# One comparison per candidate builds the one-hot rows, and candidate columns are kept batch by batch

## The chip, the core and the metric

The kernel runs on one core of one Trainium2 chip. The metric is the device time of one execution in microseconds (us); lower is better. A core has five engines with a queue of instructions each: TensorE (PE; PEld is its weight load), VectorE (DVE), ScalarE (ACT), GpSimd (POOL) and SyncE (SP, which here only issues DMAs). An engine works through its own queue in order and waits, at the head of the queue, for what another engine or a DMA has to deliver.

## What is computed

Block-causal attention over 8 batches, 8 heads, 576 positions and 64 columns a head, and behind it a mixture of 8 experts over the 4608 tokens, each of which goes to one expert. An expert takes at most 80 tokens, those with the greatest gate weights; every other row of the output is zero. Cut to what matters:

```python
scores = np.where(mask, scale * q @ k.T, -1e9)
x = softmax(scores) @ v                      # 4608 tokens x 512
expert_idx = np.argmax(x @ w_gate, axis=1)
gate_w = probs[np.arange(N), expert_idx]
for e in range(8):
    tok_idx = np.where(expert_idx == e)[0]
    if len(tok_idx) > capacity:              # capacity is 80
        keep = np.argpartition(-gate_w[tok_idx], capacity)[:capacity]
        tok_idx = tok_idx[keep]
    h = np.maximum(x[tok_idx] @ w1[e], 0.0)
    out[tok_idx] = gate_w[tok_idx, None] * (h @ w2[e])
```

## The kernel before

There are three stages.

**Attention.** 32 pairs of heads, four to a batch (batches 0 to 7), go through a software pipeline. A hand-written table (TURN, and LAST for the last pair) says in which order each engine gets its instructions. DVE takes the maxima of the scores (`max`, L693), transposes q and k (`prep`, L633) and copies PSUM; ACT takes the exponentials (`soft`, L704) and starts on a tile when `merge` (L697, DVE) has set its shift; TensorE is fed by both. Between these steps the table has slots `t`, each of which puts one step of the router on DVE: the steps of a batch stand in a list (`enqueue`), and a slot takes the next one. For the last three batches the list is: reciprocals of the sums (`recip`, L400 to L405), products with the logits (L467) and their sum `lg` (L473), maximum, first index, weight, and `placed` (L579), which writes the batch's gate weights into `Wt`. The attention's result x goes to the DRAM tensor `xs` (`store_x`, L423), for the last batch when all of it has been transposed.

**Selection** (L976 to L1134). `Wt` holds on each of 128 partitions two halves of 160 columns; a partition stands for one of 8 experts and one of 16 token residues. `max` (L981) finds the best eight of each half, of which six are kept as candidates, `max_index` (L1011) their columns. `spread` (L991) and TensorE (L1004) bring every candidate of an expert to all 16 partitions of that expert, and 12 counts (six on DVE, L1049, six on ACT, L1053) say how many others are greater: the slot of the candidate. From the slot a one-hot row of 80 is made (`OH`, L1060, by `one_hot`, three candidates to an instruction). `pick` (L1079) is the matmul of the one-hot rows with the token numbers (`RI`); its reduction `gi` (L1083) is the list of tokens. POOL then gathers the tokens' x from `xs`, one indirect DMA for each expert (L1094, `xg`), the first three at once. A second matmul (L1120) with `RG` picks the gate weights (`gsum`, `comb`). `warm(n, ...)` (L796) puts n matmuls on TensorE whose result nobody reads; the list WARM says how many stand at each place, and WARM_PICK two more.

**Experts.** For the first expert DVE divides the gathered rows into four tiles `xn0_0` to `xn0_3` (`prepare_pieces`, L1203), TensorE transposes them (L1271), ACT copies (L1272), and the first matmuls follow (L1223). For the second expert `split` does the same division into a tile `xn` (also L1203). `finish` (L1136 to L1185) makes a check and the row numbers for the scatter. The loads of further weights are issued on SP behind the first gather.

From the selection on, the order is not written by hand: a scheduler places the instructions by its own estimate of when each can start, except where `issue_after` forces one behind another. The divide of the first expert is so forced behind `comb` (L1134); the divide of the second expert (`split`) is not.

Of the kernel before, what the change touches and what calls it, by code (L numbers as in the profile page):

```python
# [7 lines left out]
F32 = mybir.dt.float32  # L8
F32R = mybir.dt.float32r
BF16 = mybir.dt.bfloat16  # L10
# [12 lines left out]
WARM = [8, 8, 5, 9, 8, 9]  # L23
START_WARM = 6
WARM_PICK = 2
# [163 lines left out]
def tile_attn_moe(ctx, tc, q, k, v, w_gate, w1, w2, capacity, out, xs=None, dbg=None):  # L189
# [87 lines left out]
    iota_s = const.tile([P, CHUNK], F32, name="iota_s")  # L277
    iota_p = const.tile([P, 1], F32, name="iota_p")
# [109 lines left out]
    class Batch:  # L388
# [189 lines left out]
        def placed(self):  # L578
            yield nc.vector.tensor_scalar(  # L579
                Wt[:, :, :, self.b, :].rearrange("p h t a -> p t a h"),  # L580
                self.tp[:, 0:8 * NT].rearrange("p (t a h) -> p t a h", t=NT, h=2),
                scalar1=-SHIFT, scalar2=None, op0=ALU.add)


    Wt = sel.tile([P, 2, NT, 8, 4], F32, name="Wt")
    if B < 8:
        nc.vector.memset(Wt, -SHIFT)
    Wf = Wt.rearrange("p h t b a -> p (h t b a)")
    NW = NT * 64
    HW = NW // 2  # L590

# [196 lines left out]
    def warm(n, wt, after=None):  # L788

        if not n:  # L790
            return
        with ExitStack() as order:
            if after is not None:
                order.enter_context(tc.issue_after(after.ins))
            for i in range(n):
                last = nc.tensor.matmul(wt.rearrange("p (a c) -> p a c", c=P), lhsT=identr,  # L796
                                        rhs=identr.unsqueeze(1).broadcast_to([P, 4, P]), start=(i == 0),
                                        stop=(i == n - 1))
        return last
# [86 lines left out]
    with tc.manual_schedule():  # L886
# [43 lines left out]
        bt.flip(NP - 1, 0, 8)  # L930
        pairs[n - 1].take("V01", "a")
# [12 lines left out]
        bt.store_x()  # L944
# [35 lines left out]
    for h in range(2):  # L980
        vec.max(cand16[:, h], Wf[:, h * HW:(h + 1) * HW])  # L981

# [3 lines left out]
    near = sel.tile([P, 2, NCAND], F32, name="near")  # L986
# [22 lines left out]
    with tc.issue_after(spreads[-1].ins):  # L1009
        for h in range(2):  # L1010
            vec.max_index(cidx[:, h], cand16[:, h], Wf[:, h * HW:(h + 1) * HW])  # L1011
# [4 lines left out]
    pool.tensor_tensor(pen, pen, iota_c[:, 0:NH].unsqueeze(1).broadcast_to([P, 2, NH]), op=ALU.add)  # L1016
    pool.tensor_scalar(pen[:, 1], pen[:, 1], scalar1=8.0 * NCAND, scalar2=1.0, op0=ALU.add, op1=ALU.mult)

    part = sel.tile([P, 3, 2, NH], I32, name="part")
    cix = cidx[:, :, 0:NH].bitcast(I32)  # L1020
    vec.tensor_scalar(part[:, 0], cix, scalar1=5, scalar2=None, op0=ALU.logical_shift_right)
    vec.tensor_scalar(part[:, 1], cix, scalar1=2, scalar2=7, op0=ALU.logical_shift_right, op1=ALU.bitwise_and)
    vec.tensor_scalar(part[:, 2], cix, scalar1=3, scalar2=None, op0=ALU.bitwise_and)
    part = part.rearrange("p k h i -> p k (h i)")
    lo_ = sel.tile([P, NCAND], F32, name="lo_")
    hi_ = sel.tile([P, NCAND], F32, name="hi_")
    RI = sel2.tile([P, NCAND, 3, E], BF16, name="RI")
    RG = sel2.tile([P, NCAND, 3, E], BF16, name="RG")
    pool.tensor_scalar(lo_, part[:, 2], scalar1=32.0, scalar2=iota_r, op0=ALU.mult, op1=ALU.add)
    pool.tensor_scalar(lo_[:, NH:], lo_[:, NH:], scalar1=16.0, scalar2=1.0, op0=ALU.add, op1=ALU.mult)  # L1030
    for k, m in ((0, 2.0 * BLK), (1, float(S))):
        pool.tensor_scalar(near[:, k], part[:, k], scalar1=m, scalar2=(-float(BLK), 0.0)[k], op0=ALU.mult, op1=ALU.add)
    pool.tensor_tensor(hi_, near[:, 0], near[:, 1], op=ALU.add)
# [5 lines left out]
    per_expert(RI[:, :, 0], hi_)  # L1039
    per_expert(RI[:, :, 1], lo_)  # L1040
    pool.tensor_copy(RI[:, :, 2], sb)

    slot = sel.tile([P, NCAND], F32, name="slot")
# [13 lines left out]
    pen_ = pen.rearrange("p h i -> p (h i)")  # L1057

    def one_hot(c0, c1):
        return vec.tensor_tensor(OH[:, c0:c1], slot[:, c0:c1].unsqueeze(2).broadcast_to([P, c1 - c0, CHUNK]),  # L1060
                                 iota_s.unsqueeze(1).broadcast_to([P, c1 - c0, CHUNK]), op=ALU.is_equal)
# [13 lines left out]
    for i in range(NCAND):  # L1075
        with ExitStack() as order:
            if i == NV:
                order.enter_context(tc.issue_after(warm(WARM_PICK, wt[:, 1], picked).ins))
            picked = nc.tensor.matmul(pick[0:CHUNK, 0:3 * E], lhsT=OH[:, i], rhs=RI[:, i].rearrange("p k e -> p (k e)"),  # L1079
                                      start=(i == 0), stop=(i == NCAND - 1))  # L1080
# [64 lines left out]
    def finish_():  # L1145
# [10 lines left out]
        vec.tensor_tensor(chk[:, E:E + 2], slot[:, NH - 1:NCAND:NH], cap.broadcast_to([P, 2]), op=ALU.is_lt)  # L1156
# [225 lines left out]
    with tc.If(again > 0):  # L1382
# [10 lines left out]
        many = gen.tile([P, NW], BF16, name="many")  # L1393
# [176 lines left out]
```

## Time and profile before

| | us |
|---|---|
| median of 3 runs (382.64 to 382.75) | 382.7 |
| the profiled execution | 382.09 |
| its span, first to last instruction | 380.4 |

| engine | busy us | share of the span |
|---|---|---|
| PE | 366.7 | 96% |
| DVE | 285.9 | 75% |
| ACT | 286.9 | 75% |
| POOL | 181.0 | 48% |

The profiled execution took 1.7 us more than its span: that lies before the first and after the last instruction. A busy share is a mean over three stages with different limits, and in the selection TensorE is kept busy by matmuls that nobody reads, so the table does not say what sets the end; the views of the section after next do.

### The profile page before, as it was taken

What the parts mean: (1) busy time and instruction counts of PE and PEld (TensorE: products, weight loads), DVE (VectorE), ACT (ScalarE), POOL (GpSimd) and SP (SyncE); (2) the same over time, 40 slices, a digit from 0 to 9 for tenths busy, and PEclk for the clock granted to TensorE, in tenths of its full rate; (3) what the DMA queues carried; (4) which work ended last, traced back from release to release, by engine and by line L of the source; (5) the groups of instructions that cost most, each with busy time, mean ns of one, the idle gap of its engine ahead of it and who ended that gap; (6) DMA issues with size and microseconds to landing.
All of it is one profiled execution on the core that took longest, in us unless ns stands there. A gap on an engine that the chain in (4) does not pass through costs nothing.

```text
span 380.4 us, 15167 instructions
## 1 busy us (share of the span) xinstructions
PE 366.7 (96%) x5973; PEld 247.5 (65%) x5973; DVE 285.9 (75%) x804; ACT 286.9 (75%) x880; POOL 181.0 (48%) x373
## 2 busy tenths in 40 slices
PE   5899999999999999999999999999999999999993
PEld 3666667676676776676676676667667555666661
DVE  5889999999999999999999999999985311111001
ACT  1799999999999999999999999999521332322331
POOL 6346665656976766786577664431133112220000
PEclk9999999999999999999999999999999999999998
DMA  9979999999999999999999999999965999999940
GB/s 125 155 122 157 141 163 152 204 188 124 190 228 146 200 197 198 165 146 247 167 171 215 184 155 137 244 396 416 264 127 175 385 391 393 401 397 393 407 188 26
DMA packets 166272, 84.42 MB, mean 222 GB/s; under 512 B 132509, under 2 KB 151805, under 8 KB 166192
## 3 DMA queue, kind: packets, MB, share of 16 engines
q1 hardware_dynamic: 154768, 61.80, 75.4%
q0 software_dynamic: 9056, 21.27, 23.9%
q8 instruction: 49, 0.80, 1.0%
q10 hardware_dynamic: 2368, 0.30, 0.6%
q14 instruction: 31, 0.25, 0.3%
HBM read 63.21 MB, written 20.33 MB: 220 GB/s over the span
## 4 chain that ended last, share of the span: by engine, by line
PE 85%; DVE 8%; ACT 3%; DMA 2%; issue 1%; POOL 0%; POOLq 0%; ACTq 0%; SPq 0%; DVEq 0%
PE bank L764 21%; PE bank L657 20%; PE bank L738 13%; PE av L1321 9%; PE ps L1236 9%; PE bank L432 2%; PE bank L769 2%; DMA ld<-in_q_dram 2%; ACT P L704 2%; DVE raw L693 2%; DVE negm L693 1%; PE ps L796 1%; PE bank L674 1%; PE pm L1321 1%; DVE T L633 1%; PE bank L446 1%
## 5 line engine op out<-in xcount | busy, mean ns | idle before, releaser
L704 ACT ACTIVATE P<-bank,negm 128x512 f32<-128x512 f32 (+3 forms) x320 | 157.2, 546 | 9.1 <-DVE negm L693 5.8
L657 PE MATMUL bank<-T,qt 64*128 64x320 f32 (+3 forms) x512 | 98.8, 494 | 0.1
L764 PE MATMUL bank<-PT,vn 128*64 128x64 f32 (+3 forms) x1288 | 88.9, 292 | 0.0
L693 DVE TENSOR_REDUCE negm<-bank 128x1 f32<-128x320 f32 (+2 forms) x192 | 83.3, 472 | 6.2 <-PE bank L683 6.1
L786 ACT COPY PT<-bank 128x512 f32<-128x512 f32 x149 | 77.0, 633 | 3.3 <-PE bank L738 2.8
L764 PEld LDWEIGHTS bank<-PT,vn 128*64 128x64 f32 x1288 | 57.1, 137 | 26.8 <-ACT PT L786 3.4
L640 POOL TENSOR_SCALAR qt<-T 128x128 f32<-128x128 f32 (+2 forms) x96 | 31.1, 342 | 89.3 <-DVE T L633 89.3
L738 PEld LDWEIGHTS bank<-ident,P 64*128 64x128 f32 (+1 forms) x1600 | 57.9, 137 | 11.7 <-issue 6.6
L738 PE MATMUL bank<-ident,P 64*128 64x64 f32 (+1 forms) x1600 | 63.4, 225 | 1.3 <-ACT P L704 0.6
L657 PEld LDWEIGHTS bank<-T,qt 64*128 64x128 f32 x512 | 47.9, 187 | 25.4 <-ACT PT L786 15.8
L704 ACT ACTIVATION_READ_ACCUMULATOR P<-bank,negm 128x1 f32 x256 | 61.0, 238 | 0.0
L693 DVE TENSOR_REDUCE raw<-bank 128x1 f32<-128x64 f32 (+1 forms) x128 | 51.7, 443 | 2.2 <-PE bank L657 1.9
L633 DVE STREAM_TRANSPOSE T<-ld 128x576 f32<-128x576 f32 x64 | 49.0, 765 | 2.8 <-DMA ld<-in_q_dram 1.6
L626 POOL DMA_DIRECT2D vn<-in_v_dram x58 | 45.8, 792 | 0.6 <-issue 0.4
L1321 PE MATMUL av<-w,hT 128*32 128x512 f32 (+3 forms) x320 | 39.3, 554 | 0.0
L618 POOL DMA_DIRECT2D ld<-in_k_dram x54 | 37.4, 699 | 2.7 <-DMA ld<-in_q_dram 2.7
L1330 DVE SCALAR_TENSOR_TENSOR y<-av,comb,yt 80x512 f32<-80x512 f32 (+1 forms) x8 | 5.6, 696 | 42.0 <-ACT yt L1328 41.9
L1236 PE MATMUL ps<-xsT,w 128*64 128x80 f32 x896 | 32.6, 233 | 0.0
L1236 PEld LDWEIGHTS ps<-xsT,w 128*64 128x64 f32 x896 | 31.4, 138 | 1.4 <-issue 0.9
L1336 POOL DMA_INDIRECT out_dram<-y,si x8 | 7.5, 942 | 51.9 <-DVE y L1330 38.8
L1328 ACT ACTIVATE yt<-ps,gfar 32x512 f32<-32x512 f32 (+2 forms) x18 | 11.4, 634 | 24.5 <-PE ps L1321 24.4
L786 DVE COPY PT<-bank 128x512 f32<-128x512 f32 x43 | 29.2, 682 | 0.3
(203 smaller groups left out, 421.2 us busy)
## 6 DMA issues: line engine op xcount, KB each, us to landing
w<-in_moe_w_dram SPq DMA_DIRECT2D x13, 2048.0 KB, 15.8
xs<-Y SPq DMA_DIRECT2D x32, 288.0 KB, 6.4
out_dram<-zero SPq DMA_DIRECT2D x18, 512.0 KB, 8.2
ld<-in_q_dram SPq DMA_DIRECT2D x126, 72.0 KB, 5.3
vn<-in_v_dram POOLq DMA_DIRECT2D x58, 128.0 KB, 4.9
w<-in_moe_w_dram POOLq DMA_DIRECT2D x12, 512.0 KB, 7.2
ld<-in_k_dram SPq DMA_DIRECT2D x72, 72.0 KB, 5.1
ld<-in_k_dram POOLq DMA_DIRECT2D x54, 72.0 KB, 6.2
```

Source lines behind the costliest of these rows:

```text
L618: eng.dma_start(self.nat[x][r], (q, k)[x][b, h0 + h, :, 32 * i:32 * i + 32] .rearrange("(g r) d -> r g d", r=32))
L626: eng.dma_start(self.vn[:, h], v[b, h0 + h, 0:512].rearrange("(j p) d -> p j d", p=P))
L633: nc.vector.transpose(t, self.nat[x].rearrange("p g d -> p (g d)"))
L640: nc.gpsimd.tensor_scalar(qb[:, to], tb[:, of], scalar1=SCALE, scalar2=1.0, op0=ALU.mult, op1=ALU.mult)
L657: nc.tensor.matmul(s[h][:, c:c + n], lhsT=q_[:, P * t - BLK:P * t + BLK], rhs=k_[:, 0:n], start=(c == 0 and g != "2"), stop=(g == "1"))
L693: nc.vector.tensor_reduce(to[:, b, h:h + 1], self.s[g][h][:, c:c + n], axis=AX.X, op=ALU.max, negate=True)
L704: nc.scalar.activation(Pt[self.i % 2][u][:, h, c1:c1 + n], self.s[g][h][:, c:c + n], AF.Exp, bias=self.negm[:, t, h:h + 1], scale=1.0, acc ...
L738: nc.tensor.transpose(pt[c][0:cols.stop - cols.start, n_ * BLK:(n_ + 1) * BLK], row[u][r, h, cols], ident[r, r])
L764: nc.tensor.matmul(a4[r] if c0 is None else av[r, BLK * c0:BLK * (c0 + b1 - b0)], lhsT=self.vn[:, h, j, :], rhs=self.PT[:, h, row, b0:b1]. ...
L786: (nc.scalar.copy if (eng or TAKE[x]) == "a" else nc.vector.tensor_copy)(*self.out.pop(x))
L1236: last = nc.tensor.matmul(dst(b)[64 * c:64 * (c + 1)], lhsT=w_[:, a, cols], rhs=x_[a], start=(a == 0), stop=(a == n - 1))
L1321: last = nc.tensor.matmul(to[col:col + s1 - s0, c0:c1], lhsT=hT[:, a, s0:s1], rhs=w_[:, a, c0:c1], start=(a == ends[0]), stop=(a == ends[1 ...
```

## The change

- The columns of `Wt` are kept batch by batch, 18 to a batch, so a half is 144 columns wide, and a column number times 32 plus the residue is the token: the arithmetic that took a column number apart (`part` on DVE, `near`, `lo_`, `hi_` on POOL) becomes one multiplication (`at`).
- When batch 5 has been placed, two more `max` find the best eight of the first six batches of each half and write them behind the 144 columns. The last `max` then reads 44 columns (two batches and those eight).
- A one-hot row is made by one instruction for each candidate, twelve instead of four with two `slot` sums ahead: `iota - count == penalty`, with the iota as bf16. The constants for it are made once, in `constants3` (seven POOL instructions and one on DVE). `finish` makes the two `slot` values that it needs itself.
- The last batch's x is stored in two parts, the first right after its transposition.
- WARM has fewer matmuls at three places, WARM_PICK is gone.

```diff
-WARM = [8, 8, 5, 9, 8, 9]
+WARM = [8, 8, 3, 7, 8, 5]
-WARM_PICK = 2
...
+    def best_early():
+        for h in range(2):
+            yield nc.vector.max(Wt[:, h, HW:HW + 8], Wt[:, h, 0:NB * early_b])
...
             fill(bt.placed, "t2")
+            if bt.b == early_b - 1:
+                fill(best_early)
...
         bt.flip(NP - 1, 0, 8)
+        bt.store_x(0, 8)
...
         bt.flip(NP - 1, 8, S // 32)
-        bt.store_x()
+        bt.store_x(8)
...
-        vec.max(cand16[:, h], Wf[:, h * HW:(h + 1) * HW])
+        vec.max(cand16[:, h], Wt[:, h, NB * early_b:])
...
-    vec.tensor_scalar(part[:, 0], cix, scalar1=5, scalar2=None, op0=ALU.logical_shift_right)
...
+    pool.tensor_scalar(at.rearrange("p (h i) -> p h i", h=2), cidx[:, :, 0:NH].bitcast(I32), scalar1=32.0, scalar2=1.0,
+                       op0=ALU.mult, op1=ALU.mult)
...
-    hot = vec.tensor_tensor(slot[:, 0:NV], cnt_v, pen_[:, 0:NV], op=ALU.add)
-    for c0 in (0, 3):
+    hot = counted
+    for i in range(NCAND):
+        h, c = divmod(i, NH)
         with tc.issue_after(hot.ins):
-            hot = one_hot(c0, c0 + 3)
...
+            hot = vec.tensor_scalar(OH[:, i], iota_b[:, h], scalar1=(cnt_v, cnt_a)[h][:, c:c + 1],
+                                    scalar2=pen[:, h, c:c + 1], op0=ALU.subtract, op1=ALU.is_equal)
...
+        slot = sel.tile([P, 2], F32, name="slot")
+        for h in range(2):
+            vec.tensor_scalar(slot[:, h:h + 1], (cnt_v, cnt_a)[h][:, NH - 1:NH], scalar1=pen[:, h, NH - 1:NH],
+                              scalar2=(1.0, 0.5)[h], op0=ALU.add, op1=ALU.mult)
```

The change moves instructions at three places of DVE's queue. The first is the selection, from the last `max` to `gi`. Before:

```order
L981 MAX cand<-Wt 128x8 x2
L991 SCALAR_TENSOR_TENSOR spread<-cand,sameR_115 128x96 x4
L1011 MAX_INDEX cidx<-cand,Wt 128x8 x2
L1021 TENSOR_SCALAR part<-cidx 128x12
L1022 TENSOR_SCALAR part<-cidx 128x12
L1023 TENSOR_SCALAR part<-cidx 128x12
L1049 TENSOR_SCALAR junk,cnt_v<-av,cand 128x192 x6
L1063 TENSOR_TENSOR slot<-cnt_v,pen 128x6
L1060 TENSOR_TENSOR OH<-slot,iota_s 128x240 x2
L1068 SCALAR_TENSOR_TENSOR slot<-cnt_a,pen 128x6
L1060 TENSOR_TENSOR OH<-slot,iota_s 128x240 x2
L1083 TENSOR_REDUCE gi<-ps 80x8
```

And now:

```order
L1001 MAX cand<-Wt 128x8 x2
L1010 SCALAR_TENSOR_TENSOR spread<-cand,sameR_115 128x96 x4
L1030 MAX_INDEX cidx<-cand,Wt 128x8 x2
L1053 TENSOR_SCALAR junk,cnt_v<-av,cand 128x192 x6
L1065 TENSOR_SCALAR OH<-iota_b,cnt_v,pen 128x80 x6
L1065 TENSOR_SCALAR OH<-iota_b,cnt_a,pen 128x80 x6
L1075 TENSOR_REDUCE gi<-ps 80x8
```

The three `part` and the two `slot` are gone, and the one-hot rows of the first six candidates stand behind the counts as six single instructions, those of the other six as six more.

The second place is DVE at the start of the experts, from the last `RG` on (`xg_6165` and `xg_6166` were the gathered rows of the first and the second expert, `xg_6168` and `xg_6169` now; `comb` the gate weights; `ids`, `vm`, `chk`, `dif` belong to `finish`). Before:

```order
L1037 TENSOR_TENSOR RG_6076<-gp_6182,sameE_114 128x12x8
L1133 TENSOR_TENSOR comb_6221<-gsum_6225 80x8
L1134 TENSOR_TENSOR comb_6221<-comb_6221,gsum_6225 80x8
L1203 TENSOR_TENSOR xn0_0_6251<-xg_6165 80x128
L1203 TENSOR_TENSOR xn0_1_6252<-xg_6165 80x128
L1203 TENSOR_TENSOR xn0_2_6253<-xg_6165 80x128
L1203 TENSOR_TENSOR xn0_3_6254<-xg_6165 80x128
L1203 TENSOR_TENSOR xn_6307<-xg_6166 80x128 x4
L1141 COPY gfar_6222<-comb_6221 32x8 x2
L1141 COPY gfar_6222<-comb_6221 16x8
L1148 CAST ids_6320<-gi_6157 80x8
```

And now:

```order
L1199 TENSOR_TENSOR xn_6306<-xg_6169 80x128 x4
L1140 CAST ids_6319<-gi_6160 80x8
L1146 TENSOR_SCALAR vm_6325,nval_6324<-cand_6059 128x12
L1150 TENSOR_SCALAR slot_6328<-cnt_v_6089,pen_6082 128x1
L1150 TENSOR_SCALAR slot_6328<-cnt_a_6090,pen_6082 128x1
L1160 MEMSET dif_6336 128x8
L1125 TENSOR_TENSOR comb_6220<-gsum_6224 80x8
L1179 TENSOR_SCALAR comb_6220<-ids_6319 80x8
L1147 TENSOR_SCALAR chk_6323<-sameE_114,nval_6324 128x8
L1152 TENSOR_TENSOR chk_6323<-slot_6328,cap_133 128x2
L1126 TENSOR_TENSOR comb_6220<-comb_6220,gsum_6224 80x8
L1199 TENSOR_TENSOR xn0_0_6250<-xg_6168 80x128
```

The second expert's divide (`xn`) has moved ahead of the first expert's, and eight small instructions of `finish` with it; with the two sums `comb`, which stood there already, ten small instructions lie between the two divides. The other three tiles of the first expert follow behind the last row.

The third place is DVE in the attention, where the products of batch 6 begin (`Y` is the end of a pair's transposition, `negm` and `raw` are maxima of the next pairs). Before:

```order
L409 STREAM_TRANSPOSE Y<-xT 128x18x32
L467 TENSOR_TENSOR prod<-bank_5653,rs 128x5x16 x2
L467 TENSOR_TENSOR prod<-bank_5654,rs 128x5x16 x2
L473 TENSOR_REDUCE lg<-prod 128x40
L693 TENSOR_REDUCE negm<-bank_5641 128x1
L786 COPY PT<-bank_5678 128x8x64
L693 TENSOR_REDUCE raw<-bank_5641 128x1
L693 TENSOR_REDUCE negm<-bank_5642 128x1
L693 TENSOR_REDUCE raw<-bank_5742 128x1
L478 TENSOR_REDUCE mx<-lg 128x5
L693 TENSOR_REDUCE raw<-bank_5642 128x1
```

And now:

```order
L423 STREAM_TRANSPOSE Y<-xT 128x18x32
L418 TENSOR_SCALAR rs<-sums 64x8
L419 RECIPROCAL rs<-rs 128x40
L481 TENSOR_TENSOR prod<-bank_5660,rs 128x5x16 x2
L481 TENSOR_TENSOR prod<-bank_5661,rs 128x5x16 x2
L710 TENSOR_REDUCE negm<-bank_5653 128x1
L803 COPY PT<-bank_5690 128x8x64
L710 TENSOR_REDUCE raw<-bank_5653 128x1
L710 TENSOR_REDUCE negm<-bank_5654 128x1
L710 TENSOR_REDUCE raw<-bank_5754 128x1
L487 TENSOR_REDUCE lg<-prod 128x40
L710 TENSOR_REDUCE raw<-bank_5654 128x1
```

A part of `recip` (L418, L419) that used to be done one pair sooner stands ahead of the products, and `lg` has moved behind a maximum of the last pair.

## Rows read from the trace of the kernel before

**Rows 1.** The chain of work that ended last: start us, us, engine, name, line.

```profile
290.94 0.78 PE ps L1223 x16
```

**Rows 2.** Busy time of one stretch: PE, PEld, DVE, ACT, POOL, PEclk, DMA, GB/s.

```profile
305.00:310.00 5.00, 5.00 (x94) 3.00 (x92) 0.00 (x0) 0.87 (x2) 1.00 (x2) 1.00 1.03 407
```

**Rows 3.** Selection, in order of time: start us, us, engine, line, operation [idle before <-releaser].

```profile
275.21 5.08 SPq L423 DMA_DIRECT2D xs<-Y  x4
...
278.46 1.43 PE L796 MATMUL ps<-identr 128*128 128x512 f32 x5
...
278.86 0.55 DVE L981 MAX8 cand<-Wt 128x8 f32<-128x160 f32 x2
...
279.33 0.75 DVE L991 SCALAR_TENSOR_TENSOR spread<-cand,sameR 128x96 f32<-128x96 f32 x4
...
279.97 0.59 PE L1004 MATMUL av<-spread,before 128*128 128x192 f32 x2
...
280.71 0.17 DVE L1021 TENSOR_SCALAR part<-cidx 128x12 int32<-128x12 int32 x1
...
281.01 0.42 DVE L1049 TENSOR_SCALAR_CACHE_REDUCE junk<-av,cand 128x192 bf16<-128x192 f32 x1
...
283.24 0.17 DVE L1063 TENSOR_TENSOR slot<-cnt_v,pen 128x6 f32<-128x6 f32 x1
...
284.49 0.17 DVE L1068 SCALAR_TENSOR_TENSOR slot<-cnt_a,pen 128x6 f32<-128x6 f32 x1 [0.33 <-ACT junk L1053]
...
284.69 0.73 DVE L1060 TENSOR_TENSOR OH<-slot,iota_s 128x240 bf16<-128x240 f32 x2
...
285.79 0.17 DVE L1083 TENSOR_REDUCE gi<-ps 80x8 int32<-80x16 f32 x1 [0.38 <-PE ps L1079]
```

**Rows 4.** In order of time, from the first gather to the first expert.

```profile
286.25 1.13 POOL L1094 DMA_INDIRECT xg<-xs,gi  x1 [3.45 <-DVE gp L1108]
...
287.68 0.99 POOL L1094 DMA_INDIRECT xg<-xs,gi  x1 [0.30 <-issue]
...
288.23 2.33 PE L796 MATMUL ps<-identr 128*128 128x512 f32 x9
...
289.50 0.90 DVE L1203 TENSOR_TENSOR xn<-xg 80x128 f32<-80x128 f32 x4 [0.52 <-DMA xg<-xs,gi]
...
290.39 0.37 PE L1271 MATMUL pm<-ident,xn 80*128 80x80 f32 x3
...
290.66 0.48 ACT L1272 COPY x<-pm 128x80 f32<-128x80 f32 x3 [2.07 <-PE pm L1271]
...
290.99 0.89 DVE L1203 TENSOR_TENSOR xn<-xg 80x128 f32<-80x128 f32 x4 [0.59 <-DMA xg<-xs,gi]
...
292.50 0.17 DVE L1148 CAST ids<-gi 80x8 f32<-80x8 int32 x1
...
292.82 0.22 DVE L1155 TENSOR_SCALAR chk<-sameE,nval 128x8 bf16<-128x8 f32 x1
```

**Rows 5.** DVE and ACT in order of time, last two pairs of the attention.

```profile
250.93 0.54 DVE L404 TENSOR_SCALAR rs<-sums 64x8 f32<-64x8 f32 x2
...
252.07 0.62 DVE L693 TENSOR_REDUCE negm<-bank 128x1 f32<-128x448 f32 x1 [0.61 <-PE bank L683]
...
255.14 0.38 DVE L405 RECIPROCAL rs<-rs 128x40 f32<-128x40 f32 x1
...
260.06 0.77 DVE L473 TENSOR_REDUCE lg<-prod 128x40 f32<-128x320 f32 x1
...
263.88 0.81 DVE L693 TENSOR_REDUCE raw<-bank 128x1 f32<-128x64 f32 x2
...
265.11 0.69 ACT L704 ACTIVATE P<-bank,negm 128x512 f32<-128x512 f32 x1 [0.19 <-DVE negm L697]
```

**Rows 6.** One-us stretches around TensorE's last matmul, columns as in rows 2.

```profile
373.00:374.00 1.00, 0.89 (x34) 0.61 (x24) 0.66 (x2) 0.69 (x3) 0.00 (x0) 1.00 0.00 0
...
377.00:378.00 1.00, 0.00 (x0) 0.00 (x0) 0.00 (x0) 0.00 (x0) 0.00 (x0) 0.64 0.28 76
```

More of the change, by code (lines that the diff above doesn't have):

```diff
@@ L277, in tile_attn_moe @@
     iota_s = const.tile([P, CHUNK], F32, name="iota_s")
+    iota_r16 = const.tile([P, 1], F32, name="iota_r16")
+    iota_b = const.tile([P, 2, CHUNK], BF16, name="iota_b")
+    order_c = const.tile([P, 2, NCAND // 2], F32, name="order_c")
+    RI = const.tile([P, NCAND, 3, E], BF16, name="RI")
     iota_p = const.tile([P, 1], F32, name="iota_p")
@@ L786, in take, with warm @@
             (nc.scalar.copy if (eng or TAKE[x]) == "a" else nc.vector.tensor_copy)(*self.out.pop(x))
-    def warm(n, wt, after=None):
+    def warm(n, wt, after=None, wide=4):
         if not n:
@@ L795, in warm @@
             for i in range(n):
-                last = nc.tensor.matmul(wt.rearrange("p (a c) -> p a c", c=P), lhsT=identr,
-                                        rhs=identr.unsqueeze(1).broadcast_to([P, 4, P]), start=(i == 0),
+                last = nc.tensor.matmul(wt[:, 0:wide * P].rearrange("p (a c) -> p a c", c=P), lhsT=identr,
+                                        rhs=identr.unsqueeze(1).broadcast_to([P, wide, P]), start=(i == 0),
                                         stop=(i == n - 1))
@@ L1015, in tile_attn_moe @@
     pool.tensor_scalar(pen, key, scalar1=0.0, scalar2=8192.0, op0=ALU.is_lt, op1=ALU.mult)
[L1016 to L1020, printed above, removed]
-    vec.tensor_scalar(part[:, 0], cix, scalar1=5, scalar2=None, op0=ALU.logical_shift_right)
[L1022 to L1027, printed above, removed]
-    RG = sel2.tile([P, NCAND, 3, E], BF16, name="RG")
[L1029 to L1033, printed above, removed]
+    pool.tensor_tensor(pen, pen, order_c, op=ALU.add)
+    at = sel.tile([P, NCAND], F32, name="at")
+    RG = sel2.tile([P, NCAND, 3, E], BF16, name="RG")
+    pool.tensor_scalar(at.rearrange("p (h i) -> p h i", h=2), cidx[:, :, 0:NH].bitcast(I32), scalar1=32.0, scalar2=1.0,
+                       op0=ALU.mult, op1=ALU.mult)
     sb = sameE.unsqueeze(1).broadcast_to([P, NCAND, E])
@@ L1037, in per_expert @@
         return eng.tensor_tensor(dst, part.unsqueeze(2).broadcast_to([P, NCAND, E]), sb, op=ALU.mult)
[L1039 to L1043, printed above, removed]
+    per_expert(RI[:, :, 0], at)
     NV = NH
@@ L1075, in tile_attn_moe @@
     for i in range(NCAND):
[L1076 to L1080, printed above, removed]
+        picked = nc.tensor.matmul(pick[0:CHUNK, 0:3 * E], lhsT=OH[:, i], rhs=RI[:, i].rearrange("p k e -> p (k e)"),
+                                  start=(i == 0), stop=(i == NCAND - 1))
     gi = sel2.tile([CHUNK, E], I32, name="gi")
@@ L1155, in finish_ @@
         vec.tensor_scalar(chk[:, 0:E], sameE, scalar1=nval, scalar2=None, op0=ALU.mult)
-        vec.tensor_tensor(chk[:, E:E + 2], slot[:, NH - 1:NCAND:NH], cap.broadcast_to([P, 2]), op=ALU.is_lt)
+        slot = sel.tile([P, 2], F32, name="slot")
+        for h in range(2):
+            vec.tensor_scalar(slot[:, h:h + 1], (cnt_v, cnt_a)[h][:, NH - 1:NH], scalar1=pen[:, h, NH - 1:NH],
+                              scalar2=(1.0, 0.5)[h], op0=ALU.add, op1=ALU.mult)
+        vec.tensor_tensor(chk[:, E:E + 2], slot, cap.broadcast_to([P, 2]), op=ALU.is_lt)
         pc = ps_m.tile([P, 512], F32, name="pm")
```

44 lines of the change are left out of this document (21 added, 23 removed).

## The prediction

> **What bounds the kernel now.** I read the chain of waits first. From the selection it goes through the comparisons to the gather of the first expert's rows and on to that expert's first matmul at 290.94 [rows 1]. From there to the end it is TensorE alone: in a stretch of the experts TensorE is busy 5.00 of 5.00 us at a granted clock of 1.00 [rows 2], while the DMAs stream weights whose loads start when the first gather has landed. So whatever moves the first matmul moves the end by as much, and a gain elsewhere is worth nothing unless it reaches that matmul. Next I read the timeline of the selection [rows 3], one operation behind another, mostly on DVE, and that from the gather to the first matmul [rows 4]; there the reader is to see how the divide of expert 0 waits for its gather, that of expert 1 for the next one, and that TensorE's unread matmuls run from 288.23 to 290.56, past the moment at which the first divided tile was there. Last, the end of the attention, where DVE sets when ACT may start [rows 5].
>
> **The selection (a gain, G).** The last `max` takes 0.55 us for two, with 160 columns each [rows 3]. If the time goes by columns, 44 instead of 160 save 0.12 us each; if it does not, nothing. TensorE's count matmuls start at 279.97; the five unread matmuls ahead of them start at 278.46 and last 1.43, to 279.89, so these held them too [rows 3]. Nine such matmuls take 2.33 us and five 1.43 [rows 3, 4], so about 0.22 each: with three they end 0.45 earlier. Both together start the matmuls 0.1 to 0.4 us earlier; I take 0.4. The three `part` end when the counts start, at 281.01 [rows 3], so without them DVE can follow TensorE. From the first count to the `slot` behind the last are 2.23 us, and the last of ACT's counts can be used at 284.49 [rows 3]. All that moves by 0.4: one-hot rows from 282.85, the last ACT count at 284.1.
>
> Then twelve one-hot rows. No row shows this instruction, 80 bf16 columns with two scalars per partition, so I bound its distance to the next. From below: the three `part`, 12 columns, 0.10 each (280.71 to 281.01). From above: the four `spread`, 96 columns of f32, 0.17 each (0.75 less the last's 0.25, by three) [rows 3]. At 0.10 the eleventh step is at 283.95 and ACT's last count at 284.1 decides; at 0.17 the last row starts at 284.7. From its start to `gi` I count 0.5: 0.2 for itself and 0.3 for one weight load and one matmul, where now three stand (0.37, from the end of `OH` at 285.42 to 285.79). So `gi` starts at 284.6 to 285.2, not at 285.79 [rows 3]: G is 0.6 to 1.2, and I take 0.9.
>
> [...]
>
> **The order on DVE (a loss).** Here the change does something that its diff doesn't show. The divide of expert 1 and ten small instructions now stand ahead of the divide of expert 0. DVE takes its queue in order, so it stands at the second gather while the rows of expert 0 lie there. All times below are less G.
> - The second gather is issued 1.43 us behind the first, and its rows are there at 290.99 [rows 4]. That is when DVE goes on.
> - Four divides of expert 1: 0.89 us [rows 4].
> - Ten small instructions. In the row of them now, six start between 292.50 and 292.82, 0.06 apart [rows 4]; where one reads what the one ahead wrote, 0.10 to 0.2 as above. Bounds 0.6 and 1.3; I take 0.85.
> - So expert 0 is divided from 290.99 + 0.89 + 0.85 = 292.73, not from 289.50 [rows 4].
> - From there to the first matmul are 1.44 us now (289.50 to 290.94), with the transposes held to 290.39 by the nine unread matmuls. With five these end long before. The third tile is divided 0.42 + 0.28 after the start, the transposes take 0.37 for three, and a copy on ACT lies between the transpose and the matmul (0.27 and 0.28 us from start to start) [rows 4]: about 1.0.
> - First matmul at 293.73 - G instead of 290.94: 2.79 - 0.9 = 1.9 us later (1.3 to 2.6).
>
> The shorter warming is worth 0.4 us in this, though not its cover: what is late next is the divide.
>
> **The attention (a loss, A).** The two early `max` (108 columns, under 0.3 us each by the 0.55 for two of 160) fall behind batch 5's `placed`, where DVE then waits 0.61 us for TensorE [rows 3, 5]: nothing. But they take two slots, and the batch list slips. One `rs` of the pair 0.54 for two and the reciprocal, 0.38 [rows 5], now come right ahead of the products of batch 6, 0.5 us more on DVE; and `lg`, which held DVE from 260.06 to the next start 0.67 later, now stands between the maxima at 263.8 [rows 5]. Behind these stands `merge`, and ACT's exponential at 265.11 waits for it by the trace [rows 5]. It comes 0.57 later (0.67 less the 0.10 of `mx`, which leaves that place). I take A = 0.5; bounds 0 (hidden by TensorE, busy then too) and 0.6.
>
> **Costed at nothing.** The split store: the last x lands at 280.29 (275.21 + 5.08), the gather starts at 286.25 [rows 3, 4], so six us cover it, and the four further issues on SP stand ahead of weight loads that wait for the first gather anyway. Seven POOL instructions and one on DVE (0.1 to 0.17 by the rows above) in pair 7 lie beside TensorE's work; q, k and v are loaded pairs ahead. POOL's shorter arithmetic: it has the token numbers before the one-hot rows either way. The matmuls taken out between the two halves of `pick` stood where TensorE waited for `OH`. If the covers are gone, each costs some tenths, inside the range.
>
> **The sum.** Against the profiled execution, 382.09 us: + 1.9 + 0.5 = 384.5. The median of the runs, 382.7, is 0.6 above it, so 385.1 there.
>
> **The rivals.**
> - *The order on DVE does not hold* (faster). If the second gather is there when DVE reaches its divide, expert 0 loses little, and the change gives what it is made of: G 0.9 and 0.4 of warming, less A 0.5, so 0.8 better: 381.9. The point from which it decides is the landing of the second gather: for no loss it has to be 2.4 us sooner. Against it: the first lands 3.25 us after its issue with nothing else on the way, and the second is issued 1.43 later [rows 4]. Chance 0.06.
> - *TensorE's clock falls* (slower still). Between the five unread matmuls (end at 288.23 + 1.45 = 289.7, less G) and the first transpose (0.35 behind 292.73, less G) TensorE does nothing for 3.4 us. [...] If it falls, the first expert starts at half speed; the stretch 290.94 to 294.3 at half costs up to 3.4 us, and half of that if the clock comes back midway: 386.8 to 388.5. [...] Chance 0.22. [...]
> - *About as before*: A nothing, G at its upper end, the ten instructions at their lower, and the second gather sooner than it is now by half a us: 383.2. Chance 0.06.
>
> **How the numbers follow.** Forecast 0.66, at 385.1, its own range 383.9 to 386.0; clock 0.22; no loss 0.06; as before 0.06. The range 383.8 to 387.8 leaves out the two on the lower side, 0.12, and the upper third of the clock's. What a measurement can tell from no change is about 0.2%, 0.8 us. So faster 0.06, same 0.06, slower 0.88.
>
> **What would show it.** In the profile after, DVE's divide of expert 1 ends its wait by the second gather ahead of that of expert 0, which starts some 2.3 us later than 289.50; the first gather is issued near 285.3; the first expert's matmul starts near 293.3 (290.94 + 1.9 + 0.5), and the experts behind it keep their pace. Twelve one-hot rows stand 0.10 to 0.17 apart. The attention's end is 0.5 later. It would be wrong if the first divide starts before the second gather has landed, or if the granted clock near 293 is not 1.00.

## The result, and the profile after

The changed kernel takes 387.95 us (median of 6 runs, 386.67 to 389.56); the kernel before, run beside it, 382.73 (6 runs, 382.44 to 383.59). The ratio of the runs is 1.0137, with a 95% interval of 1.0112 to 1.0162: slower, by about 5.2 us. The forecast was 385.1 with a range up to 387.8; the sign is right and the size is not. The mean granted clock of TensorE is 0.982 to 0.990 in the six runs (0.990 in the profiled one); the 26 runs of the kernel before that stand beside e1 to e4 read 0.994 to 0.998.

The profiled execution took 388.58 us with a span of 386.9. Cut at four points that both traces show, the 6.5 us between the two spans are:

| from | to | before, us | after, us | difference |
|---|---|---|---|---|
| start | last write into `Wt` (end of the attention) | 278.60 | 280.94 | +2.34 |
| last write into `Wt` | `gi` (the list of tokens) | 7.19 | 7.15 | -0.04 |
| `gi` | first matmul of the first expert | 5.15 | 7.82 | +2.67 |
| first matmul | the next group of that expert's matmuls, 64 matmuls on | 3.32 | 5.53 | +2.21 |
| there | end of the span | 86.14 | 85.46 | -0.68 |

Two rows of before that do not stand ahead of the prediction serve as cuts, the last write into `Wt` and the group of matmuls behind the first 64 of the first expert; between them stand the last 48 of the 64 (columns as in [rows 3]):

```profile
278.60 0.23 DVE L579 TENSOR_SCALAR Wt<-bank 128x40 f32<-128x40 f32 x1 [0.27 <-PE bank L573]
...
292.06 1.83 PE L1223 MATMUL ps<-x,w 128*64 128x80 f32 x48
...
294.26 1.95 PE L1236 MATMUL ps<-x,w 128*64 128x80 f32 x50
```

The selection of after, against [rows 3]:

```profile
280.94 0.23 DVE L593 TENSOR_SCALAR Wt<-bank 128x36 f32<-128x36 f32 x1 [0.27 <-PE bank L587]
...
281.20 0.31 DVE L1001 MAX8 cand<-Wt 128x8 f32<-128x44 f32 x2
...
283.14 0.42 DVE L1053 TENSOR_SCALAR_CACHE_REDUCE junk<-av,cand 128x192 bf16<-128x192 f32 x1 [0.37 <-PE av L1023]
...
283.99 0.42 ACT L1057 ACTIVATE junk<-ps,keyn 128x192 bf16<-128x192 f32 x1 [5.02 <-DMA xs<-Y]
...
285.17 1.36 DVE L1065 TENSOR_SCALAR OH<-iota_b,cnt_v,pen 128x80 bf16<-128x80 bf16 x6
...
286.44 1.35 DVE L1065 TENSOR_SCALAR OH<-iota_b,cnt_a,pen 128x80 bf16<-128x80 bf16 x6
...
288.09 0.17 DVE L1075 TENSOR_REDUCE gi<-ps 80x8 int32<-80x16 f32 x1 [0.30 <-PE ps L1071]
```

To the first count it is 2.20 us from the last write, where before needed 2.41 (the two `max` take 0.31, where they took 0.55), and from the first count to the first one-hot row 2.03 where it was 2.23 to `slot`. Both savings are there. The twelve rows take them back: from the first row to `gi` 2.92, where before went from `slot` to `gi` in 2.55. The seventh row starts 1.27 behind the first, so they stand 0.21 apart.

From the first gather to the first expert, against [rows 4], and the clock (columns as in [rows 2]):

```profile
288.55 1.12 POOL L1086 DMA_INDIRECT xg<-xs,gi  x1 [5.05 <-DVE gp L1100]
...
289.98 0.99 POOL L1086 DMA_INDIRECT xg<-xs,gi  x1 [0.30 <-issue]
...
290.53 1.40 PE L813 MATMUL ps<-identr 128*128 128x512 f32 x5
...
293.19 0.89 DVE L1199 TENSOR_TENSOR xn<-xg 80x128 f32<-80x128 f32 x4 [3.25 <-DMA xg<-xs,gi]
294.00 0.16 DVE L1140 CAST ids<-gi 80x8 f32<-80x8 int32 x1
...
294.85 0.89 DVE L1199 TENSOR_TENSOR xn<-xg 80x128 f32<-80x128 f32 x4
...
295.19 0.80 PE L1267 MATMUL pm<-ident,xn 80*128 80x80 f32 x3 [3.25 <-DVE xn L1199]
...
295.91 1.34 PE L1219 MATMUL ps<-x,w 128*64 128x80 f32 x16
...
297.83 3.25 PE L1219 MATMUL ps<-x,w 128*64 128x80 f32 x48
...
301.44 0.78 PE L1232 MATMUL ps<-x,w 128*64 128x80 f32 x16
```

```profile
292.00:293.00 1.00, 0.00 (x0) 0.00 (x0) 0.00 (x0) 0.00 (x0) 0.23 (x1) 1.00 0.51 125
293.00:294.00 1.00, 0.00 (x0) 0.00 (x0) 0.81 (x4) 0.00 (x0) 0.00 (x0) 0.97 0.74 120
294.00:295.00 1.00, 0.00 (x0) 0.00 (x0) 1.00 (x13) 0.00 (x0) 0.00 (x0) 0.50 0.97 374
...
300.00:301.00 1.00, 1.00 (x20) 0.91 (x16) 0.00 (x0) 0.00 (x0) 0.00 (x0) 0.62 0.92 352
```

DVE waits 3.25 us for the second gather, divides expert 1 (293.19), does the small instructions (294.00), and only then divides expert 0 (294.85). TensorE has nothing to do from 291.93 to 295.19; in that idle time, near 294 and so some 2.0 us behind its last matmul, its clock goes to 0.50 of full speed, and it comes back only near 300.8 (0.62 as the mean of 300 to 301). At half clock 48 matmuls take 3.25 us; before they took 1.83.

In the attention three places move (before, then after, for the first; TensorE in pair 16, and DVE and ACT in the last pair, for after):

```profile
102.03 0.97 POOL L640 TENSOR_SCALAR qt<-T 128x128 f32<-128x128 f32 x3 [0.54 <-DVE T L633]
```

```profile
102.49 0.97 POOL L657 TENSOR_SCALAR qt<-T 128x128 f32<-128x128 f32 x3 [0.87 <-DVE T L650]
...
140.40 0.21 PE L755 MATMUL bank<-ident,P 64*64 64x64 f32 x1 [1.30 <-issue]
...
265.59 0.73 DVE L487 TENSOR_REDUCE lg<-prod 128x40 f32<-128x320 f32 x1
...
267.46 0.69 ACT L721 ACTIVATE P<-bank,negm 128x512 f32<-128x512 f32 x1 [0.20 <-DVE negm L714]
```

`merge` runs 0.1 us later than before up to the pair at 109 us, 0.3 more from the next pair on (called pair 13 below; pairs count from 0), 1.2 more from pair 16 on, and 0.7 more in the last (pair 31): 2.35 together. The last step is the slip of the batch list: `lg` now stands at 265.59 ahead of `merge`.

### The profile page after: what moved, and what is told of

Read it like the earlier page. It is cut to its first block, busy times and chain, and to the rows that moved or that the text cites. A ratio compares the mean times of both kernels' runs of the same rounds, so it can differ in the third digit from the quotient of the medians.

```text
span 386.9 us, 15156 instructions
## 1 busy us (share of the span) xinstructions
PE 368.1 (95%) x5963; PEld 248.5 (64%) x5963; DVE 286.0 (74%) x812; ACT 287.3 (74%) x880; POOL 181.5 (47%) x373
## 4 chain that ended last, share of the span: by engine, by line
PE 81%; DVE 6%; DMA 6%; issue 2%; ACT 2%; SPq 2%; POOL 0%; POOLq 0%; ACTq 0%; DVEq 0%
PE bank L781 20%; PE bank L674 19%; PE bank L755 12%; PE av L1317 10%; PE ps L1232 9%; PE bank L446 2%; DMA xs<-Y 2%; DMA ld<-in_q_dram 2%; PE bank L786 2%; ACT P L721 2%; DVE negm L710 1%; DVE raw L710 1%; SPq L437 1%; PE ps L1219 1%; DMA ld<-in_k_dram 1%
```

## Experiments

Each part of the forecast was taken out or put in by itself. Ratios are to runs of the kernel before beside them on the same chip; they are not the quotients of the medians. What is said of a trace holds for one execution.

### The divide of expert 0 ahead again (e1)

The changed kernel, with expert 1's divide forced behind that of expert 0:

```diff
-        divided_[e] = divide(xn_[e], xg[e])
+        with ExitStack() as order:
+            if e == 1:
+                order.enter_context(tc.issue_after(divided_[0].ins))
+            divided_[e] = divide(xn_[e], xg[e])
...
-            divide(xn, xg[0])
+            divided_[0] = divide(xn, xg[0])
```

> The kernel after with one edit: the divide of expert 1 is forced behind that of expert 0, as it stood before. Theory 'order': of the 5.2 us that the median lost, the place of that divide on DVE cost 3.1 us (first divide at 294.85 in the profile after, first gather landed near 291.8) and the fall of TensorE's clock behind it 2.2 us (the first expert's 64 matmuls took 5.1 us from 295.9 to 301.0, and 2.9 us before). Both go: 387.95 - 5.3 = 382.6, granted clock 1.00 until the last matmul. Rival 'attention': the loss is mostly what the profile after shows ahead of the selection (2.3 us at the last batch's router), and the order on DVE is covered by the gathers; then about 385.5 here.

Measured: 383.38 us, ratio 0.9999 (0.9972 to 1.0027): the loss is gone. In its trace the divide of expert 0 is released by its own gather and the first matmul follows 0.97 later; the clock stays at 1.00.

```profile
288.63 1.13 POOL L1086 DMA_INDIRECT xg<-xs,gi  x1 [5.05 <-DVE gp L1100]
...
291.77 0.89 DVE L1199 TENSOR_TENSOR xn<-xg 80x128 f32<-80x128 f32 x4 [0.41 <-DMA xg<-xs,gi]
...
292.74 0.78 PE L1219 MATMUL ps<-x,w 128*64 128x80 f32 x16
```

The two theories that it was to tell apart gave 382.6 and 385.5, and it stands by the first. It is no faster than before, so the rest of the change gives back what it wins: from the divide to the first matmul it is 0.97 instead of 1.44, with the shorter warming, and the shifts of the attention are in this trace too (pair 13 by 0.3, the last pair by 0.7, and 1.2 in pair 16).

### The same order put into the kernel before (e2)

The kernel before, with only the divide of expert 1 forced ahead of that of expert 0:

```diff
+            split(1)
+        with tc.issue_after(divided_[1].ins):
```

> The kernel before with one edit: the divide of expert 1 is forced ahead of that of expert 0; nothing else of the change is in it. Theory 'order': expert 0 is divided when the second gather has landed and four divides of 0.22 us are over, 291.9 instead of 289.5, and with TensorE's unread matmuls out of the way the first matmul comes 1.9 us later: 382.7 + 1.9 = 384.6. TensorE is idle for 1.7 us only, so the clock stays. Rival 'attention': within 0.5 us of the kernel before.

Measured: 386.36 us, ratio 1.0059 (1.0017 to 1.0102). From the first gather's issue to the first matmul it is 6.56 us instead of 4.69: 1.87 lost, and 1.9 was expected. The time is 2.3 us longer by the ratio (0.7 to 3.9). What was not expected is that the clock falls here as well, though TensorE's idle time is only 1.63 us:

```profile
293.45 0.69 PE L1273 MATMUL pm<-ident,xn 80*128 80x80 f32 x3 [1.63 <-DVE xn L1203]
294.07 0.78 PE L1223 MATMUL ps<-x,w 128*64 128x80 f32 x16
...
295.33 3.28 PE L1223 MATMUL ps<-x,w 128*64 128x80 f32 x48
```

```profile
293.00:294.00 1.00, 0.55 (x3) 0.41 (x3) 1.00 (x5) 0.22 (x2) 0.00 (x0) 1.00 0.99 382
294.00:295.00 1.00, 1.00 (x18) 0.76 (x17) 0.88 (x10) 0.41 (x3) 0.00 (x0) 0.96 1.01 385
295.00:296.00 1.00, 1.00 (x15) 0.99 (x16) 0.16 (x2) 0.23 (x1) 0.00 (x0) 0.50 1.01 406
```

When it falls, near 295, TensorE has been at work again for more than a microsecond. The 48 matmuls lose 1.45. It need not fall in every execution: the mean granted clock of the seven runs is 0.991 to 0.999, 0.994 in the profiled one, and the three runs at 0.997 and above are the three shortest (383.19, 383.60 and 385.48 of 383.19 to 387.69). This trace also has a delay in pair 16, of 0.65 us, and it is before's own code there.

### More warming in the changed kernel (e3)

```diff
-WARM = [8, 8, 3, 7, 8, 5]
+WARM = [8, 8, 3, 7, 8, 20]
```

> The kernel after with one edit: 20 unread matmuls instead of 5 ahead of the first expert's transposes, so that TensorE is busy until its first divided tile is there. The order on DVE stays. Theory 'order, then clock': the divide is as late as in the kernel after, but the clock stays at 1.00 and the first expert's matmuls take 2.9 us again: 387.95 - 2.2 = 385.7. Rival 'the clock is no loss of its own' (the first expert waits for something else anyway): 387.9.

Measured: 386.74 us, ratio 1.0128 (1.0080 to 1.0177, four runs): this lies between the 385.7 and the 387.9 of the two theories, and by the times it cannot be told from the changed kernel. By the trace it does what it was meant to: the clock stays at 1.00 and the 48 matmuls take 1.83 again, while the wait for the second gather stays (3.23).

```profile
289.38 4.82 PE L813 MATMUL ps<-identr 128*128 128x512 f32 x20
...
292.02 0.89 DVE L1199 TENSOR_TENSOR xn<-xg 80x128 f32<-80x128 f32 x4 [3.23 <-DMA xg<-xs,gi]
...
294.63 0.78 PE L1219 MATMUL ps<-x,w 128*64 128x80 f32 x16
...
295.75 1.83 PE L1219 MATMUL ps<-x,w 128*64 128x80 f32 x48
```

From the first matmul to the next group it is 3.32 us, as in before, so the 2.2 us are back; behind that 0.7 are lost again (86.15 us to the end of the span, 85.46 in after), 0.5 of it before the second expert starts. With 1.2 less in the attention the span is 384.1, 2.8 under that of after. That the clock is worth as much in the time, e3 does not show.

### No early maximum (e4)

e1 without the two early `max`; the last `max` reads all 144 columns.

```diff
-            if bt.b == early_b - 1:
-                fill(best_early)
...
-        vec.max(cand16[:, h], Wt[:, h, NB * early_b:])
+        vec.max(cand16[:, h], Wf[:, h])
```

> As e1_order, and without the early search of the best eight of six batches: the last max reads all 144 columns. Theory 'slip': the two steps more in the batch list put the sum of the products between the last pair's maxima (0.7 us at that place in the profile after), while the wider last max costs 0.2 us: 0.45 us below e1_order, and the last pair's exponential stands to the pair before it as in the kernel before. Rival: the slip is hidden, so this is 0.2 us above e1_order.

Measured: 382.42 us, ratio 0.9980 (0.9961 to 1.0000); the times do not tell it from e1, the trace does. The last pair is no later than the one ahead of it (before + 1.09 and + 1.10): the slip of 0.71 belongs to the early `max`. The last two maxima cost 0.52 instead of 0.31, so the early ones win 0.21 in the selection and lose 0.71 ahead of it.

```profile
261.16 0.75 DVE L487 TENSOR_REDUCE lg<-prod 128x40 f32<-128x320 f32 x1
...
266.20 0.69 ACT L721 ACTIVATE P<-bank,negm 128x512 f32<-128x512 f32 x1 [0.20 <-DVE negm L714]
...
279.95 0.52 DVE L999 MAX8 cand<-Wt 128x8 f32<-128x144 f32 x2
```

### What a one-hot row costs (e5, e6)

Both start from e4. e5 adds count and penalty ahead, so that a row has one scalar per partition; e6 keeps two scalars and makes the iota f32 instead of bf16.

```diff
-            hot = vec.tensor_scalar(OH[:, i], iota_b[:, h], scalar1=(cnt_v, cnt_a)[h][:, c:c + 1],
-                                    scalar2=pen[:, h, c:c + 1], op0=ALU.subtract, op1=ALU.is_equal)
+            hot = vec.tensor_tensor(sums_[:, h], (cnt_v, cnt_a)[h], pen[:, h], op=ALU.add)
+        for c in range(NH):
+            with tc.issue_after(hot.ins):
+                hot = vec.tensor_scalar(OH[:, NH * h + c], iota_b[:, h], scalar1=sums_[:, h, c:c + 1], scalar2=None,
+                                        op0=ALU.is_equal)
```

```diff
-    iota_b = const.tile([P, 2, CHUNK], BF16, name="iota_b")
+    iota_b = const.tile([P, 2, CHUNK], F32, name="iota_b")
```

> As e4_no_early_max, but the count and the penalty of six candidates are summed first (two instructions of 128x6), so that a one-hot instruction reads one scalar per partition instead of two; all else of it, 80 bf16 columns, stays. In the profile after, twelve with two scalars stand 0.225 us apart. Theory 'second scalar': the second one costs it, and with one they stand 0.13 to 0.17 apart. Rival 'a price per instruction': still 0.20 or more; then gi comes 0.3 to 0.4 us later than in e4_no_early_max, counted from the last write of Wt (7.32 us there, 7.19 before).

> As e4_no_early_max, but the iota that the one-hot instructions read is f32 instead of bf16; two scalars, as there. Theory 'second scalar' and theory 'a price per instruction': the distance stays at 0.225 us, or grows by less than 0.06. Rival 'bf16 input is what costs': it falls to 0.17, the distance of the 96 f32 columns of the spread.

The first six rows of e5, then of e6; those of e4 take 1.36 us as in the changed kernel:

```profile
284.18 0.99 DVE L1066 TENSOR_SCALAR OH<-iota_b,sums__6115 128x80 bf16<-128x80 bf16 x6
```

```profile
283.80 1.47 DVE L1063 TENSOR_SCALAR OH<-iota_b,cnt_v,pen 128x80 bf16<-128x80 f32 x6
```

Six rows take 0.99 us with one scalar, 1.36 with two, and 1.47 with two and f32; from start to start they stand 0.15, 0.21 and 0.23 apart. So the second scalar and its operation cost more than a quarter of the row, and the type little. Which of the two it is, e5 does not separate, since its rows have one operation instead of two. That an operation alone costs little is likely from the trace of before: the three `part` start at 280.71, 280.80 and 280.90, and the next instruction at 281.01. All three have constants and no scalar per partition, only the middle one has two operations, and its step of 0.10 is no longer than the third's. As a kernel e5 (382.6, a single run) wins nothing: from the last write into `Wt` to `gi` it is 7.31 us against 7.32 in e4, since the two sums stand ahead of the rows. e6 (382.9, a single run) needs 7.59.

### Three candidates to an instruction (e7)

e4 with the one-hot rows made three at a time, as before did, on the bf16 iota, and ACT's six sums in two halves:

```diff
+    for h, c0, c1 in ((0, 0, 6), (1, 0, 3), (1, 3, 6)):
...
+        for c in range(c0, c1, 3):
+            with tc.issue_after(hot.ins):
+                hot = vec.tensor_tensor(OH[:, NH * h + c:NH * h + c + 3],
+                                        sums_[:, h, c:c + 3].unsqueeze(2).broadcast_to([P, 3, CHUNK]),
+                                        iota_b[:, h].unsqueeze(1).broadcast_to([P, 3, CHUNK]), op=ALU.is_equal)
```

> A version meant to beat both: as e4_no_early_max (order on DVE as before, no early max, token arithmetic and warming of the change), but the one-hot rows are made three candidates to an instruction again, and ACT's six candidates in two halves, the first of which does not wait for ACT's last count. Theory 'one-hot rows are the selection's price': gi at 6.7 us from the last write of Wt (7.32 in e4_no_early_max, 7.19 before; DVE is free some 0.3 us before ACT's last count), and with the 0.45 us of warming 0.8 to 0.9 us below the kernel before in the same state of the attention: 381.8 to 382.3 against 382.7. Rival: the gather's landing hides it, ratio within 0.1% of e4_no_early_max.

Measured: 381.15 us, ratio 0.9949 (0.9921 to 0.9977): faster than both kernels. Six rows take 0.73 us, and from `Wt` to `gi` it is 6.93 (6.7 was expected). A part is lost again in this trace: the clock falls behind the picks, `comb` comes late, and the divide of expert 0 waits for it and not for its gather. From `gi` to the first matmul that makes 5.53 us, against 5.15 in before. The gain of 0.9 to 3.0 us in the times is thus more than the 0.26 that this trace, of one of the longer runs (382.09), shows in the selection. Nine of the twelve runs have a mean granted clock of 0.996 or more, this one 0.993, so the fall need not be in them; where the rest comes from is open.

```profile
283.96 0.73 DVE L1066 TENSOR_TENSOR OH<-sums__6115,iota_b 128x240 bf16<-128x240 f32 x2
...
285.92 3.21 PE L813 MATMUL ps<-identr 128*128 128x512 f32 x8
286.10 0.17 DVE L1077 TENSOR_REDUCE gi<-ps 80x8 int32<-80x16 f32 x1 [0.38 <-PE ps L1073]
...
290.12 0.16 DVE L1127 TENSOR_TENSOR comb<-gsum 80x8 f32<-80x8 f32 x1 [2.17 <-ACT gsum L1126]
...
290.40 1.82 DVE L1201 TENSOR_TENSOR xn<-xg 80x128 f32<-80x128 f32 x8
```

### The constants made later (e8)

e7 with the eight constant instructions of the change moved from pair 7 to pair 24:

```diff
+    def constants4():
...
+            if i == 24:
+                constants4()
```

> As e7_thirds, with the eight constant instructions (seven on POOL, one on DVE) in pair 24 instead of pair 7. In every kernel so far with the change, pair 13 ends 0.3 us later than in the two kernels without it, at a DVE transpose that waits for a load of k which POOL issued. Theory 'constants': POOL's work in pair 7 shifted the loads that it issues, so the 0.3 us are gone at pair 13 here (or appear some pairs behind 24). Rival 'another cause' (placement of tiles, or chance): pair 13 is still 0.3 us later.

Measured: 381.01 us, ratio 0.9960 (0.9927 to 0.9993). In its trace the step of 0.3 us at pair 13 is gone, and none stands behind pair 24. The time does not tell it from e7; the trace does. All eight traces with the constants in pair 7 have the step, and the four without (before, e2, e8, e9) do not. The eight instructions (seven on POOL) at pair 7 are thus what costs 0.3 six pairs later, where POOL starts 0.3 late on a tile that DVE has finished (in the rows of pair 13 above). What delays POOL there the trace does not show.

### Matmuls between the picks again (e9)

```diff
-WARM = [8, 8, 3, 7, 8, 5]
+WARM = [8, 8, 3, 9, 8, 5]
...
+            if i == NH:
+                order.enter_context(tc.issue_after(warm(2, wt[:, 1], picked).ins))
```

> e8 with two unread matmuls put back between the first six and the last six picks of the one-hot rows, as before had them, and nine instead of seven behind the ranking: nothing else differs. Theory (TensorE's clock falls in the selection because the thirds leave it sparse work, small picks with gaps, and fewer unread matmuls): the granted clock stays 1.00 from 284 to 290, where e8 shows 0.50 to 0.79; the eight unread matmuls behind the picks take about 2 us instead of 3.41, comb is there some 1.4 us sooner, and the first divide is released by its gather, some 0.6 us sooner behind the selection; the two matmuls delay the last picks by at most 0.3. Time 380.2 to 380.8, 0.3 to 0.8 under e8. Rival (the clock falls whatever stands there, or the gather is what ends last in any case): the same time as e8, 381.0, or 0.3 more.

Measured: 380.61 us, ratio 0.9949 (0.9930 to 0.9968): the lowest median here, two us under before, though the times do not tell it from e7 and e8. The clock in one stretch of e8, then of e9, and the rows of e9 that answer it:

```profile
286.00:287.00 1.00, 1.00 (x4) 0.71 (x3) 0.56 (x3) 0.00 (x0) 0.69 (x2) 0.50 0.00 0
```

```profile
286.00:287.00 1.00, 1.00 (x6) 0.82 (x5) 0.90 (x6) 0.00 (x0) 1.00 (x1) 1.00 0.00 0
```

```profile
285.32 2.11 PE L816 MATMUL ps<-identr 128*128 128x512 f32 x8
...
289.16 0.89 DVE L1209 TENSOR_TENSOR xn<-xg 80x128 f32<-80x128 f32 x4 [0.45 <-DMA xg<-xs,gi]
```

The eight unread matmuls take 2.11 us (3.41 in e8), the divide is released by its gather, and from the last write into `Wt` to that divide it is 10.59 us instead of 11.35. Its attention ended 0.7 later than that of e8, by a wait of TensorE in pair 16; that is why the two spans are alike (379.0 and 378.9). That the matmuls keep the clock up in every execution is not shown: no run of e9 has a mean granted clock under 0.995, but of e8's ten runs five are above 0.994 too (0.988 to 0.998 in all).

### The changed kernel again (e10)

> The changed kernel once more, for a second trace. Theory: what belongs to the kernel comes again, to 0.1 us: the first twelve one-hot rows 0.225 apart, the divide of the first expert behind the second gather, the clock at 0.50 behind 294, pair 13 of the attention 0.3 and pair 31 0.7 later. What does not belong to it is the wait of 1.3 us of TensorE in pair 16 that no other engine or DMA releases: it may be anything from 0 to 1.3 us, and the span is 386.9 less what it is shorter. Rival (the wait is the kernel's): 1.3 us again, and span 386.9.

Measured: 391.22 us (a single run), span 389.5, where at most 386.9 was expected. What belongs to the kernel comes again: six one-hot rows in 1.35, the divide of expert 0 behind the second gather, 0.3 at pair 13, 0.7 in the last pair, the clock near 0.50 from 297 on. The wait of TensorE in pair 16 is 0.80 (it was 1.30), and in pair 26 there is one of 1.60 that the first trace does not have, behind a load that came late:

```profile
139.26 0.21 PE L755 MATMUL bank<-ident,P 64*64 64x64 f32 x1 [0.80 <-issue]
```

```profile
223.24 0.78 DVE L650 STREAM_TRANSPOSE T<-ld 128x576 f32<-128x576 f32 x1 [2.18 <-DMA ld<-in_k_dram]
...
227.14 0.83 PE L691 MATMUL bank<-T,qt 64*64 64x64 f32 x8 [1.60 <-POOL qt L657]
```

Here the clock also fell in pair 27 (0.50 at 229 to 232) and in the selection, behind the picks (0.50 at 291 to 293), which it did not in the first trace of the same kernel. So delays come and go in the attention from one execution to the next, in this one of some 4 us (0.75 in pair 16, 3.25 in pairs 26 and 27). The wait in pair 16 is in the kernel before's code too: 0.09 us in its own trace, 0.74 in e2. Whether the change makes it longer on average is open; with the constants in pair 7 it is 0.25 to 1.30 in eight traces.

## Why the prediction was wrong, and where it was right

The forecast had a loss of 2.4 us, and what is the kernel's own is 5.9 in the traces (the sum below). The step that failed most is the clock, which the sum left at 1.00 for the first expert: 2.2 us. Next comes the distance of the one-hot rows, and with it G: 0.9. The attention adds 0.5: the slip 0.2 more than taken, and 0.3 for the constants, which stood at nothing.

**The order on DVE: right.** The divide of expert 0 stands behind the second gather, the four divides of expert 1 (0.89, as taken) and the ten small instructions (294.00 to 294.85, 0.85 as taken); 1.06 later follows the first matmul (1.0 taken). Without G, 2.79 was forecast, and it is 2.67 in the trace. e1 takes the order back and the loss goes with it; e2 puts it alone into the kernel before and loses 1.87 up to the first matmul.

**The selection, G: wrong.** 0.9 was taken, 0.6 to 1.2 given as bounds, and it is 0.04. The first row starts where it was put (285.17 less the attention's 2.34 is 282.83, and 282.85 was worked out). The step that failed is the distance of the rows: 0.17, that of the four `spread`, stood as the upper bound, and they stand 0.21 apart, so that the eleven steps take 2.3 us instead of 1.1 to 1.9. From the last row's start to `gi` it is 0.6, where 0.5 was counted; the row itself takes 0.30 and not 0.2. Neither of the two rows that gave the bounds is an instruction with two scalars per partition, and with one scalar and one operation less the distance is 0.15, inside the bounds (e5).

**The clock: the wrong case was called likeliest.** The rival of the clock gave 386.8 to 388.5, and the time is 387.95. Its price was right: the first 64 matmuls lose 2.2 us, between the 1.7 and the 3.4 of its working, and e3 takes them back with the clock alone. The half speed that it reckons with is in no row of [rows 6], where 0.64 is the lowest; the traces show it, 0.50 from 378 to 380 in before and from 294 to about 300.8 in after. That the time lies inside the rival's is in part luck: with the clock's 2.2 alone the sum is 387.3; G and the attention put some 1.3 more on it, and 0.7 comes back behind the first 64 matmuls. Wrong was the chance of 0.22, and with it the upper end of the range, 387.8, which cut off the last two fifths of the rival's prices and not a third. The idle time was forecast well (3.4, and 3.25 by the trace). At the end of before's span the clock fell some 3.4 us behind the last matmul, an estimate from the 0.64 of [rows 6] and the 0.50 that follows it. In after it fell sooner, some 2.0 us behind the last matmul: it reads 0.97 from 293 to 294 and 0.50 from 294 on, while TensorE is still idle. That is the sign of being wrong that the prediction named, a granted clock near 293 that is not 1.00. In e2 it falls behind an idle time of 1.63, when the work has begun again. What one fall at the end of the span shows ([rows 6]) did not carry over to another place. When the work has begun again (295.19), the clock of after stays at 0.50 for another 5.6 us, and the first expert's matmuls run in that time.

**The attention, A: too small, and a price of nothing that was not nothing.** The slip was seen and put at 0.57, taken as 0.5; it is 0.71 (after, e1, e3, e10; gone in e4). The constants in pair 7, costed at nothing, cost 0.3 (gone in e8). They were priced at 0.1 to 0.17 each by rows of DVE; seven of them are POOL's, which needs about 1.6 us for these (72.93 to 74.50 in after), and POOL issues loads too (two of k from 75.08). The remaining 1.2 of the profiled execution is the wait in pair 16, which changes from run to run (e10) and shows in before's code as well (e2).

**The sum of what is the kernel's own:** 0.7 and 0.3 in the attention, 2.63 from its end to the first matmul and 2.21 for the clock are 5.9 us, where the forecast had 2.4; the medians are 5.2 apart. What stands between is of the size of what changes from trace to trace without the change: the rest of the first expert, up to the second's start, takes 7.96 us in after, e1, e2 and e8, 8.31 in before and 8.47 in e3. Why, was not tried.

**Right at nothing:** the split store and POOL's shorter arithmetic. One wait in the trace is put down to the store, that of ACT's first count (283.99, `DMA xs<-Y`), but the count starts 0.08 behind the end of TensorE's matmuls for it, as in before, so it did not wait for the store. The cover was misread all the same. The 5.08 us behind 275.21 are SP's issuing; the last store was issued at 278.65 and landed 5.6 us later, at 284.3, which leaves 2.0 us to the first gather and not six. In after it landed at 285.7, and 2.9 us are left. **Open** are the matmuls taken out between the two halves of `pick`, which also stood at nothing: in the first trace of after the clock stays at 1.00 in the selection, in e10 it falls there.

## What to carry to other kernels

When an edit adds or removes steps on an engine whose order a scheduler sets, compare the order of the instructions first: here a divide that changed places cost more than all that the edit was made of could win (387.95 us with it, 383.38 without, e1). An idle stretch of TensorE ahead of its long work is to be priced with the clock (3.25 us idle, and 2.2 lost behind it, in after), or to be filled with matmuls (with 15 more the clock stayed at 1.00 there, e3). And a row of the trace need not bound an instruction that reads other kinds of operands: the 0.17 us of `spread` did not bound a row with two scalars, 0.21.

## What the runs showed of the hardware that was not expected

- A `tensor_scalar` of 128 x 80 in bf16 with two scalars per partition comes every 0.21 us on DVE; six take 1.36 us, with one scalar and one operation less 0.99, with two scalars and f32 1.47.
- TensorE's clock went to 0.50 in an idle time of 3.25 us, 2.0 us behind the last matmul (after), and behind one of 1.63 with the work already begun again (e2, one trace). It also went there without a long pause (0.50 us is the longest that the rows of e5 to e8 name there), among or right behind twelve small matmuls with gaps between them (e5 to e8, where 8 unread matmuls took 3.2 to 3.6 us instead of 2.1, and e10), but not in the traces of after, e1, e3 and e4, which have such matmuls too. With two unread matmuls between the picks and two more ahead of them it stayed at 1.00 (e9, one trace).
- TensorE waited 0.09 to 1.30 us in the same place of pair 16, with no releaser that the trace shows, in all twelve traces and in both kernels' code. Its cause was not tried.
